# Moving parts of a chunked linear attention between four engines: scores to ScalarE and GpSimd, states and diagonals to VectorE

## The chip, the cores and the metric

The kernel runs on one core of a Trainium2 chip. The metric is device time in microseconds (us). The engines are TensorE (PE in the rows, its weight loads PEld), VectorE (DVE), ScalarE (ACT), GpSimd (POOL) and SyncE (SP), which issues nearly all loads and stores. Each engine works through its own queue in order and waits on semaphores for the others.

## The reference

Three layers follow each other. The first is a linear attention with a decaying state per head, the other two are feed-forward layers, the last one with a router over eight experts.

```python
# 4 batches, 8 heads, 768 steps, head size 48
for t in range(S):
    cur = einsum('bhd,bhe->bhde', u * k[t], v[t])
    y[t] = einsum('bhd,bhde->bhe', r[t], state + cur)
    state = w * state + einsum('bhd,bhe->bhde', k[t], v[t])
x = y as 3072 tokens x 384
h = x @ w_in                       # 384 -> 2048
g = h where h >= 1, 0 where h <= -1, else (h + 1)**2 / 4
x = g @ w_out                      # 2048 -> 384
# router: argmax of normalised x with 8 experts, gate = its softmax value
out = gate * (relu(x @ w1[e]) @ w2[e])   # 384 -> 1024 -> 384
```

## The kernel before

The 3072 tokens are 24 units of 128 steps, six to a batch. A unit works on its steps at once: the decay goes into r and k beforehand (`rk`), the scores of all steps with all steps are taken by TensorE (`s0`) into two PSUM tiles of 128x512 with four heads each, evacuated with a mask that keeps the steps before (`e0`, `e1`, function `s0_ev`), and multiplied with v (`s1`), to which the state of the unit before is added by further matmuls. What a step gives itself, the term with u, is the diagonal of the scores, a number per step and head (`dg`, `dg2`). For units below `DIAG` (8) it is multiplied with v apart (`dv`, on VectorE for the first four units and on GpSimd for units 4 to 7), and TensorE adds it into the output of `s1` by three transposes. For later units it is written into the diagonal of the masked scores by a predicated copy on VectorE (`dd`, function `s0_dg`, two instructions a unit), and the transposes fall away.

The state after a unit is the old one plus k times v, with the decay of 128 steps put on it. For units below `BY_PE` (5) TensorE also adds the old state, by a matmul with the identity, and ScalarE evacuates the sum with the decay as its scale (`s2p`). For later units TensorE gives only k times v, VectorE adds the old state in two instructions (`s2v`) and ScalarE puts the decay on in four (`s2w`). The last unit of a batch makes no state.

ScalarE and VectorE split the output of a unit into a high and a low part (`s3h`, `s3l`) for the first feed-forward layer, which takes three matmuls for each product. Six blocks of 512 tokens go through it in steps of 128 hidden columns: `h` on TensorE, four operations on ScalarE and one on VectorE, the low part `gl` on GpSimd, then `o` and `og` on TensorE. The weights come in as packed 64-bit numbers and are unpacked on the way, in three instructions on VectorE, one on ScalarE and one on GpSimd (`wlo`), in time for their first use. Units 0 to 7 are the first two blocks; later units are slipped in between the steps of earlier blocks.

The order on every engine is written out ahead by a planner, class `Schedule`. Each task has an engine, a modelled length (`COST`), what it depends on, what buffers it takes, and a due time. The planner goes forward in modelled time and gives an engine, of the tasks that are ready first, the one with the earliest due time. `SHIFT` adds an offset to the due time, by kind (`"e0"`), by unit or step (`"u3"`, `"k17"`) or by both (`"s1_u8"`). The PSUM tiles of the attention share five slots (`att`). Before the first matmuls that count, TensorE is kept busy by matmuls with the identity (L761).

Lines of the profile that the text names: `s0` L616 (units below 8) and L624, `e0`/`e1` L636, `dd` L653, `dv` L605, transposes of dv L694, `s1` L690, state by TensorE L715 and L720, without it L724, its evacuation L680, `s2v` L735 and L737, `s2w` L743, `rk` L541, `kk` L550, `ru` L566 and L568, `wlo` L481, `gl` L854.

Of the kernel before, what the change touches and what calls it, by code (L numbers as in the profile page):

```python
# [15 lines left out]
AF = mybir.ActivationFunctionType  # L16
ALU = mybir.AluOpType
# [7 lines left out]
C = 128  # L25
NU = NT // C
UPB = S // C
NP = H // 2
# [2 lines left out]
NF2 = F2 // 128  # L31
WARM = 9
RAMP = 4
DIAG = 8
HALVES = 2
ROLL = 8
W_LO, W_HI = 0.75, 1.3125
# [25 lines left out]
class Schedule:  # L63
# [47 lines left out]
    def run(self):  # L111
# [63 lines left out]

COST = {"wkc": 0.42, "s2p": 1.0, "dg": 0.12, "s3h": 0.4, "whi": 0.76, "relu": 0.59, "over": 0.53, "sqr": 0.53, "gh": 0.53,
# [58 lines left out]
def d_pe(n):  # L235
    return n / 2300 + 0.011


SHIFT = {"": 31.25, "az": 14, "b0": -19.75, "b1": -26, "b2": 4.5, "b3": 22.75, "b4": -30.5, "b5": 295.25, "dd":
# [15 lines left out]
         "le0": -5.75, "le1": -39.25, "le2": -6.75, "lka": 9.25, "lkl": -20.5, "lkm": -9.5, "look": -248.5, "max":  # L255
# [14 lines left out]
         46.25, "sm": 330, "sma": -190, "smc0": -63.25, "smc1": 0.25, "sqa": -87.25, "sqs": -32.25, "swd": -3.5,  # L270
# [8 lines left out]
         "whp": 6.5, "wkc": -2.75, "wkd": -3.25, "wkr": 6.75, "wl": 109.75, "wlo": 201.5, "wlp": -72.5, "wp1": 25.25,  # L279
         "wp2": 35.25, "wp3": 54.5, "x1ld": 28.75, "x2h": 30.5, "x2l": 36, "x2ld": -14.25, "xth0": -21, "xth1": 8,  # L280
         "xtl0": -57.75, "xtl1": -6.25, "xts0": -46.5, "xts1": -3.5, "xts2": -54.75, "xts3": 7.25, "z": 98.5, "zs":
         -119.75}
U_DVE, U_PE, W_DVE = 4.7, 3.5, 4.0
ON_DVE = {}
KK_PE, W_PSUM, G_PSUM, DV_PSUM, BY_PE = 2, 2, 0, 4, 5


@with_exitstack
def fused_kernel(ctx, tc, att, wcol, wrow, ub, ucol, win, wout, emb, tau, w1, w2, out):
    nc = tc.nc  # L290
# [42 lines left out]
    def bcast(ap, shape):  # L333
        return ap.to_broadcast(shape)
# [143 lines left out]
    def w_lo(c, eng=None):  # L478
# [8 lines left out]
                            channel_multiplier=-1)  # L487
# [26 lines left out]
    ats = [atp.tile([128, 2, NP, C], F32, name=f"at{i}") for i in range(2)]  # L514
# [6 lines left out]
    st = {}  # L521
# [110 lines left out]
    def s0_ev(u, j):  # L632
        s = st[u]
        at = s["at"] = ats[u % 2]
        if u < ROLL:
            nc.vector.tensor_tensor(out=at[:, j], in0=s["a"][j], in1=bcast(mask.unsqueeze(1), [128, NP, C]), op=ALU.mult)  # L636
        else:
            m = C // 2
            nc.vector.tensor_tensor(out=halves(at[:, j, :, m:]), in0=halves(s["a"][j][:, :, m:]),
                                    in1=bcast(sel[:, 0, :, m:].unsqueeze(2), [128, 2, NP // 2, m]), op=ALU.mult)  # L640
            for i in range(2):
                x, y = slice(m * i, m * i + m), slice(2 * i, 2 * i + 2)
                nc.vector.tensor_tensor(out=at[x, j, y, 0:m], in0=s["a"][j][x, y, 0:m],
                                        in1=bcast(sel[x, 0, i:i + 1, 0:m], [m, NP // 2, m]), op=ALU.mult)

    def s0_dg(u, j):
        s = st[u]
# [656 lines left out]
    add = sch.add  # L1304
# [23 lines left out]
    for u in range(NU):  # L1328
# [49 lines left out]
        e0 = add("e0", f"u{u}", "DVE", 0.68, lambda u=u: s0_ev(u, 0), [s0] + z + (sels if u >= ROLL else []), due - 9,  # L1378
                 alloc=[] if z else [atb], use=[a0] + ([atb] if z else []), after=e0s[u - 2:u - 1] if u > 1 else [])
        e0s.append(e0)  # L1380
        e1 = add("e1", f"u{u}", "DVE", 0.68, lambda u=u: s0_ev(u, 1), [s0, e0], due - 9, use=[a1, atb])
        if u >= DIAG:
            dv = dg
            for j in range(2):
                dv = add("dd", f"u{u}", "DVE", 0.62, lambda u=u, j=j: s0_dg(u, j), [e1, dv], due - 4.5, use=[atb, dgb])
        c = u % UPB
        s1 = add("s1", f"u{u}", "PE", (2.2 if c else 1.75) - 0.45 * (u >= DIAG), lambda u=u: (xt_tiles(unit_blk[u][0]), s1_pe(u)),
                 [e1, dv, l1, s2e.get(u - 1) if c else None, xhu.get(4 * m)], due - 1.5,
                 alloc=[yb] + (list(xbuf[m]) if i == 0 else []),
                 use=[ab, atb] + ([dvb] if u < DIAG else []) + ([state_b[u - 1]] if c else []) + (list(xbuf[m]) if i else []),  # L1390
                 after=[s1_of[u - 1]] if u else [])
# [562 lines left out]
```

## Time and profile before

| what | value |
| --- | --- |
| median of 3 runs | 710.27 us (709.94 to 710.44) |
| the profiled execution | 710.95 us |
| its span, first to last instruction | 709.1 us |
| granted clock of TensorE | 1.00 |
| TensorE busy | 699.4 us |
| VectorE busy | 450.4 us |
| ScalarE busy | 416.7 us |
| GpSimd busy | 304.8 us |

The profile is of one execution. Busy times are unions of the instructions of an engine. Matmuls are pipelined, their durations overlap and their ends are modelled, so the time that a group of them takes is read from its start to the start of the next group. The chain that ended last is followed back from the last instruction, at each step to what released it or to the instruction before it on its engine.

### The profile page before, as it was taken

The page shows a single profiled execution, that of the slowest core. Times are in us where ns is not written, and L with a number is a line of the kernel's source. Part 1 is how long each engine was busy: PE and PEld are TensorE (multiplying, and loading weights), DVE is VectorE, ACT ScalarE, POOL GpSimd, SP SyncE. Part 2 cuts the span into 40 slices and gives each one's busy share as a digit, 9 for nine tenths or more (in the row PEclk, how much of TensorE's full clock was granted, in tenths as well). Part 3 has the DMA queues.
Part 4 walks back from the last instruction along what each step waited for, and adds up shares of the span by engine and source line. Part 5 has one row for each costly group of instructions (what it writes and reads, how often), then busy time and mean ns, then how long its engine had stood idle before and what let it go on. Part 6 is the DMA issues. An engine that isn't in the chain of part 4 may idle for free.

```text
span 709.1 us, 14241 instructions
## 1 busy us (share of the span) xinstructions
PE 699.4 (99%) x5743; PEld 597.2 (84%) x5743; DVE 450.4 (64%) x842; ACT 416.7 (59%) x744; POOL 304.8 (43%) x251
## 2 busy tenths in 40 slices
PE   8999999999999999999999999999999999999997
PEld 7788888877888888887787888887899999999996
DVE  7989987699998313235994512121588586948664
ACT  3357777566556557765756866676566364625432
POOL 4699996574476522333622322234561121112100
PEclk9999999999999999999999999999999999999999
DMA  7866445254455105322642302000412021102011
GB/s 261 321 207 209 175 155 175 67 169 161 154 176 179 65 1 177 111 91 89 221 154 86 94 0 90 1 0 1 152 35 81 3 90 44 47 0 90 6 41 48
DMA packets 26136, 74.93 MB, mean 106 GB/s; under 512 B 2505, under 2 KB 9682, under 8 KB 26066
## 3 DMA queue, kind: packets, MB, share of 16 engines
q1 hardware_dynamic: 25778, 73.59, 30.8%
q8 instruction: 46, 0.75, 0.5%
q10 hardware_dynamic: 288, 0.39, 0.2%
q14 instruction: 24, 0.20, 0.1%
HBM read 62.74 MB, written 11.01 MB: 104 GB/s over the span
## 4 chain that ended last, share of the span: by engine, by line
PE 89%; DVE 4%; POOL 2%; DMA 2%; issue 1%; ACT 1%; POOLq 0%; DVEq 0%; SPq 0%
PE psh L341 9%; PE psh L343 9%; PE psh L342 9%; PE acc L876 9%; PE acc L879 9%; PE acc L877 9%; PE o L1246 5%; PE o L1243 5%; PE o L1244 5%; PE psm L341 4%; PE psm L342 4%; PE psm L343 4%; PE psy L690 3%; DMA attn<-att 2%; PE psa L624 2%; PE pslt L1009 1%
## 5 line engine op out<-in xcount | busy, mean ns | idle before, releaser
L854 POOL TENSOR_TENSOR gl<-a,gh 128x512 fp32r<-128x512 f32 (+1 forms) x98 | 136.8, 1397 | 185.5 <-ACT gh L849 171.5
L845 DVE TENSOR_TENSOR a<-psh,a 128x512 f32<-128x512 f32 (+1 forms) x98 | 66.5, 679 | 148.3 <-ACT a L842 146.5
L876 PE MATMUL acc<-gh,wout_h 128*128 128x512 f32 (+1 forms) x294 | 116.5, 398 | 0.1
L341 PE MATMUL psh<-xh,win_h 128*128 128x512 f32 (+1 forms) x294 | 115.6, 393 | 0.0
L343 PE MATMUL psh<-xh,win_l 128*128 128x512 f32 (+1 forms) x294 | 114.9, 391 | 0.0
L342 PE MATMUL psh<-xl,win_h 128*128 128x512 f32 (+1 forms) x294 | 114.9, 391 | 0.0
L877 PE MATMUL acc<-gh,wout_l 128*128 128x512 f32 (+1 forms) x294 | 114.5, 391 | 0.0
L835 ACT ACTIVATE a<-psh,half 128x512 f32<-128x512 f32 (+1 forms) x98 | 66.3, 676 | 73.1 <-PE psh L343 64.7
L849 ACT ACTIVATE gh<-a 128x512 fp32r<-128x512 f32 (+1 forms) x98 | 60.6, 620 | 42.4 <-DVE a L845 38.4
L1203 DVE TENSOR_TENSOR sc<-sc,psm 128x256 f32<-128x256 f32 x176 | 64.1, 417 | 30.5 <-PE psm L343 20.4
L879 PE MATMUL acc<-gl,wout_h 128*128 128x512 f32 (+1 forms) x294 | 82.3, 393 | 0.2 <-POOL gl L854 0.2
L876 PEld LDWEIGHTS acc<-gh,wout_h 128*128 128x128 f32 x294 | 55.2, 188 | 15.0 <-ACT a L842 1.0
L341 PEld LDWEIGHTS psh<-xh,win_h 128*128 128x128 f32 x294 | 55.2, 188 | 13.0 <-issue 0.2
L343 PEld LDWEIGHTS psh<-xh,win_l 128*128 128x128 f32 x294 | 55.2, 188 | 12.8
L342 PEld LDWEIGHTS psh<-xl,win_h 128*128 128x128 f32 x294 | 55.2, 188 | 12.5
L879 PEld LDWEIGHTS acc<-gl,wout_h 128*128 128x128 f32 x294 | 54.3, 188 | 13.3 <-POOL gl L854 0.4
L877 PEld LDWEIGHTS acc<-gh,wout_l 128*128 128x128 f32 x294 | 55.3, 188 | 11.9
L1243 PE MATMUL o<-w2h,gh 128*128 128x384 f32 x192 | 64.6, 336 | 0.0
L1244 PE MATMUL o<-w2l,gh 128*128 128x384 f32 x192 | 64.4, 336 | 0.0
L839 ACT ACTIVATE a<-a 128x512 f32<-128x512 f32 (+1 forms) x98 | 60.9, 621 | 2.5
L842 ACT ACTIVATE a<-a 128x512 f32<-128x512 f32 (+1 forms) x98 | 60.7, 619 | 2.2
L1218 ACT ACTIVATE gh<-sc 128x512 fp32r<-128x512 f32 x44 | 26.7, 627 | 47.2 <-DVE sc L1203 43.7
(218 smaller groups left out, 1387.3 us busy)
## 6 DMA issues: line engine op xcount, KB each, us to landing
att<-att SPq DMA_DIRECT2D x22, 736.0 KB, 5.1
w<-win SPq DMA_DIRECT2D x16, 768.0 KB, 5.2
w<-wout SPq DMA_DIRECT2D x16, 768.0 KB, 4.5
attn<-att SPq DMA_DIRECT2D x20, 384.0 KB, 3.9
x1d<-x SPq DMA_DIRECT2D x6, 768.0 KB, 4.8
x1f<-x1d SPq DMA_DIRECT2D x6, 768.0 KB, 5.8
out<-o SPq DMA_DIRECT2D x10, 384.0 KB, 2.9
hw<-w SPq DMA_DIRECT2D x8, 384.0 KB, 4.0
```

Source lines behind the costliest of these rows:

```text
L341: nc.tensor.matmul(o, lhsT=sh, rhs=mh, start=first, stop=False, skip_group_check=True)
L342: nc.tensor.matmul(o, lhsT=sh, rhs=ml, start=False, stop=False, skip_group_check=True)
L343: nc.tensor.matmul(o, lhsT=sl, rhs=mh, start=False, stop=last, skip_group_check=True)
L835: nc.scalar.activation(out=a, in_=hp, func=AF.Relu, bias=half[:, 0:1], scale=0.5)
L845: nc.vector.tensor_tensor(out=a if out is None else out, in0=hp, in1=a, op=ALU.max)
L854: (eng or nc.gpsimd).tensor_tensor(out=gl, in0=a, in1=gh.bitcast(F32), op=ALU.subtract)
L876: nc.tensor.matmul(o, lhsT=wh, rhs=gh, start=(f == f0 and c0 == 0), stop=False, skip_group_check=True)
L877: nc.tensor.matmul(o, lhsT=wl, rhs=gh, start=False, stop=False, skip_group_check=True)
L879: nc.tensor.matmul(o, lhsT=wh, rhs=gl, start=False, stop=(f == f1 - 1), skip_group_check=True)
L1203: nc.vector.tensor_tensor(out=out, in0=x, in1=bank[:, j], op=op)
L1243: nc.tensor.matmul(o, lhsT=gh[:, c], rhs=ws[2][:, f, :], start=(f == 0), stop=False, skip_group_check=True)
L1244: nc.tensor.matmul(o, lhsT=gh[:, c], rhs=ws[3][:, f, :], start=False, stop=False, skip_group_check=True)
```

## The change

Half of the scores of units 0 to 3, the four heads of `e1`, are evacuated by ScalarE as a plain copy (`ea`, new function `s0_copy`) and masked in place by GpSimd with an `affine_select` (`em`, new function `s0_mask`); `E_ACT` says for how many units. `BY_PE` goes from 5 to 3, so the states of units 3 and 4 take the form of the later units; `DIAG` goes from 8 to 6, so the diagonals of units 6 and 7 do. The wait of `s1` on `e0` is named beside that on `e1`. The small loads for the tables of the router (`mixl`) wait for `s1` of unit 5 in place of unit 7, as they follow `DIAG`. `COST` gets the two new kinds, and all of `SHIFT` is new; its values are left out here.

```diff
-DIAG = 8
+DIAG = 6
...
+"ea": 0.53, "em": 1.23,
...
-SHIFT = {"": 31.25, "az": 14, "b0": -19.75, "b1": -26,
...
+SHIFT = {"": 48.75, "az": 10.5, "b0": 14.25, "b1": -32,
...
+E_ACT = 4
 U_DVE, U_PE, W_DVE = 4.7, 3.5, 4.0
 ON_DVE = {}
-KK_PE, W_PSUM, G_PSUM, DV_PSUM, BY_PE = 2, 2, 0, 4, 5
+KK_PE, W_PSUM, G_PSUM, DV_PSUM, BY_PE = 2, 2, 0, 4, 3
...
+    def s0_copy(u, j):
+        nc.scalar.activation(out=ats[u % 2][:, j], in_=st[u]["a"][j], func=AF.Copy)
+
+    def s0_mask(u, j):
+        at = ats[u % 2][:, j]
+        nc.gpsimd.affine_select(out=at, in_=at, pattern=[[0, NP], [1, C]], compare_op=ALU.is_gt, fill=0.0, base=0, channel_multiplier=-1)
...
-        e1 = add("e1", f"u{u}", "DVE", 0.68, lambda u=u: s0_ev(u, 1), [s0, e0], due - 9, use=[a1, atb])
+        if u < E_ACT:
+            e1 = add("ea", f"u{u}", "ACT", 0, lambda u=u: s0_copy(u, 1), [s0, e0], due - 9, use=[a1, atb])
+            e1 = add("em", f"u{u}", "Pool", 0, lambda u=u: s0_mask(u, 1), [e1], due - 9, use=[atb])
+        else:
+            e1 = add("e1", f"u{u}", "DVE", 0.68, lambda u=u: s0_ev(u, 1), [s0, e0], due - 9, use=[a1, atb])
...
-                 [e1, dv, l1, s2e.get(u - 1) if c else None, xhu.get(4 * m)], due - 1.5,
+                 [e0, e1, dv, l1, s2e.get(u - 1) if c else None, xhu.get(4 * m)], due - 1.5,
```

## Rows read from the trace of the kernel before

**Rows 1.** The page: the span, and busy time, share and instructions of each engine.

```profile
span 709.1 us, 14241 instructions
PE 699.4 (99%) x5743; PEld 597.2 (84%) x5743; DVE 450.4 (64%) x842; ACT 416.7 (59%) x744; POOL 304.8 (43%) x251
```

**Rows 2.** Stretches: from:to, length, busy us of each engine (instructions), clock, DMA.

```profile
8.00:28.00 20.00, 18.67 (x311) 15.04 (x309) 19.14 (x32) 6.66 (x19) 8.67 (x8) 1.00 0.88 338
28.00:57.00 29.00, 28.73 (x516) 24.33 (x509) 25.82 (x44) 15.88 (x40) 27.43 (x27) 1.00 0.67 222
57.00:104.00 47.00, 47.00 (x206) 38.10 (x207) 42.41 (x38) 35.23 (x59) 44.98 (x28) 1.00 0.51 172
...
380.00:704.00 324.00, 323.76 (x1922) 291.48 (x1920) 174.64 (x397) 181.47 (x310) 87.93 (x77) 1.00 0.15 46
704.00:709.10 5.10, 0.00 (x0) 0.00 (x0) 0.59 (x1) 0.10 (x1) 0.00 (x0) 1.00 0.43 154
```

**Rows 3.** Waits of TensorE: line and what it waited for, total us, times, longest.

```profile
PE psy L694 <- DVE at L636: 0.7, 1, 0.7
```

**Rows 4.** The chain that ended last, in order of time: start us, us, what.

```profile
19.29 8.34 DMA attn<-att
...
51.24 0.69 POOL gl L854
...
52.90 2.02 POOL dv L605 x2
...
54.97 0.33 PE psy L694
```

**Rows 5.** Timeline of TensorE: start us, us, instruction, how many merged.

```profile
28.11 0.91 PE L715 MATMUL pskv<-state,ident 128*128 128x384 f32 x2
...
29.45 0.55 PE L694 MATMUL psy<-ident,dv 128*128 128x128 f32 x3
...
46.52 0.52 PE L724 MATMUL pskv<-att,kk 128*32 128x48 f32 x32
46.98 0.39 PE L876 MATMUL acc<-gh,wout_h 128*128 128x256 f32 x1
...
49.92 0.49 PE L694 MATMUL psy<-ident,dv 128*128 128x128 f32 x3
50.34 1.08 PE L690 MATMUL psy<-at,att 128*32 128x128 f32 x32
```

**Rows 6.** VectorE, 0 to 140 us, groups: count, busy us, mean ns, idle before.

```profile
L636 DVE TENSOR_TENSOR at<-psa,mask 128x512 f32<-128x512 f32 x16 | 10.3, 682 | 0.0
...
L735 DVE TENSOR_TENSOR state<-pskv,state 48x192 f32<-48x192 f32 x4 | 1.4, 352 | 4.5 <-PE pskv L724 4.4
```

**Rows 7.** Tile `at`: count, ns at least, median, most, first and last start.

```profile
L653 DVE COPY_PREDICATED at<-sel,dg x32: 722/760/2377, 135.7 to 370.3; 128x512 f32<-128x512 int32 x32
```

**Rows 8.** GpSimd, 0 to 140 us, groups, columns as in group 6.

```profile
L605 POOL TENSOR_TENSOR dv<-att,dg 128x256 f32<-128x256 f32 x4 | 4.8, 1191 | 0.0
...
L605 POOL TENSOR_TENSOR dv<-att,dg 128x128 f32<-128x128 f32 x4 | 2.4, 590 | 0.0
...
L486 POOL TENSOR_SCALAR_AFFINE_SELECT mask<-mask 128x128 f32<-128x128 f32 x1 | 0.3, 292 | 0.1
```

**Rows 9.** ScalarE, 0 to 140 us, groups, columns as in group 6.

```profile
L885 ACT ACTIVATE x<-acc 128x512 f32<-128x512 f32 x4 | 2.2, 596 | 0.1
```

**Rows 10.** Timelines of VectorE and GpSimd near 38 us, columns as in group 5.

```profile
38.02 1.21 DVE L541 TENSOR_TENSOR att<-att,pwt 128x1024 f32<-128x1024 f32 x1
...
36.98 1.01 POOL L566 TENSOR_TENSOR ru<-attn,ubt 128x384 f32<-128x384 f32 x1 [0.37 <-DVE dg L589]
38.07 2.04 POOL L568 TENSOR_TENSOR ru<-ru,attn 128x384 f32<-128x384 f32 x1
```

**Rows 11.** Timelines of GpSimd and TensorE near 60 us, columns as in group 5.

```profile
58.52 1.83 POOL L481 TENSOR_TENSOR wout_l<-sc,wout_h 128x768 fp32r<-128x768 f32 x1
...
62.26 0.40 PE L876 MATMUL acc<-gh,wout_h 128*128 128x512 f32 x1
```

More of the change, by code (lines that the diff above doesn't have):

```diff
@@ L236, in d_pe @@
     return n / 2300 + 0.011
-SHIFT = {"": 31.25, "az": 14, "b0": -19.75, "b1": -26, "b2": 4.5, "b3": 22.75, "b4": -30.5, "b5": 295.25, "dd":
[15 rows of a table removed]
-         "le0": -5.75, "le1": -39.25, "le2": -6.75, "lka": 9.25, "lkl": -20.5, "lkm": -9.5, "look": -248.5, "max":
[14 rows of a table removed]
-         46.25, "sm": 330, "sma": -190, "smc0": -63.25, "smc1": 0.25, "sqa": -87.25, "sqs": -32.25, "swd": -3.5,
[8 rows of a table removed]
[L279 to L282, printed above, removed]
+SHIFT = {"": 48.75, "az": 10.5, "b0": 14.25, "b1": -32, "b2": 8, "b3": 24.25, "b4": -39.75, "b5": 244.25, "dd":
[16 rows of a table added]
+         "lka": 12.5, "lkl": -20.5, "lkm": -25, "look": -239.5, "max": -71.75, "mixl": 33.75, "o": 294.5, "o2": 53.5,
[14 rows of a table added]
+         -9.25, "sm": 403.25, "sma": -190.75, "smc0": 0.75, "smc1": -37, "sqa": -1.5, "sqr": 15, "sqs": -2, "swh":
[8 rows of a table added]
+         0.5, "wkd": 14.25, "wkr": 110.5, "wl": 113.25, "wlo": 219.5, "wlp": -213.5, "wp1": 27.5, "wp2": -8.25,
+         "wp3": 139.5, "x1ld": 27.25, "x1st": 14.75, "x2h": 67.75, "x2l": 26.75, "x2ld": -19.25, "xth0": -33.25,
+         "xth1": 53.5, "xtl0": -132.75, "xtl1": 0.5, "xts0": -11, "xts1": 85.75, "xts2": -24, "xts3": 3.75, "z":
+         98.75, "zs": -147}
+E_ACT = 4
 U_DVE, U_PE, W_DVE = 4.7, 3.5, 4.0
 ON_DVE = {}
-KK_PE, W_PSUM, G_PSUM, DV_PSUM, BY_PE = 2, 2, 0, 4, 5
+KK_PE, W_PSUM, G_PSUM, DV_PSUM, BY_PE = 2, 2, 0, 4, 3
 @with_exitstack
```

77 rows, old and new, of tables (COST, SHIFT) are left out of this document.

## The prediction

> **What bounds the kernel now.** I read the page's totals first, then the busy time by stretch, then the waits of TensorE, then the chain that ended last, and only then single rows. The totals show TensorE busy for 699.4 us of a span of 709.1 [rows 1], so at most 9.7 us of the span are not its work. The stretches say where these lie [rows 2]: from 57 us to 704 us it has next to no idle time, after 704 us come 5.1 us of evacuation and stores that the change does not touch, from 8 to 28 us it is idle for 20 - 18.67 = 1.33 us, and from 28 to 57 us for 0.27 us. The rest lies ahead of 8 us, where nothing of this change runs. So the time is the start, TensorE's own work, some 1.6 us of waits in the attention of the first two blocks, and the tail. A change can win by taking work off TensorE, or by taking away these waits; it can lose only by making new ones.
>
> The same two stretches show how little room the others have there [rows 2]. VectorE is busy for 19.14 of 20 us and then 25.82 of 29; GpSimd for only 8.67 of 20, but then 27.43 of 29, and 44.98 of 47 after that; ScalarE for 6.66 of 20 and 15.88 of 29. The longest wait of TensorE in the first stretch, 0.7 us, ends with VectorE's masking of scores [rows 3]. The chain that ended last runs up to 55 us through others: 8.34 us of a load that lands at 27.6 us, and in its last piece GpSimd's gl, kk and then 2.02 us of dv of unit 7, which releases the transposes of that unit [rows 4]. From there on it is TensorE. So up to 55 us several engines are near their limit at once, and an order of the work has to suit all of them.
>
> **The change, part by part. TensorE.** With `BY_PE` 3 the states of units 3 and 4 are no longer carried by TensorE. For unit 3 this group starts at 28.11 us with the identity matmul and the next one, the transposes, at 29.45: 1.34 us. The form without the identity starts at 46.52 us for unit 6, and the next matmul at 46.98: 0.46 us [rows 5]. Unit 4 repeats unit 3, so the saving is 2 x 0.88 = 1.76 us. With `DIAG` 6 the three transposes of dv of units 6 and 7 go; those of unit 6 take from 49.92 to 50.34 us [rows 5], 0.42 us, twice 0.84. Together TensorE loses 2.60 us, all of it inside a stretch in which it is never idle for long. I count from start to start, since the durations in the rows overlap.
>
> **VectorE.** It loses the second half of the masks of units 0 to 3, 4 x 0.68 = 2.73 us [rows 6], all before 28 us. It gains two adds for each of two states, 4 x 0.35 = 1.42 us [rows 6], and four predicated copies for the diagonals of units 6 and 7. The trace has these copies only for later units: 0.72 us at best, 0.76 in the median, 2.38 at worst [rows 7]. I take 0.76, the median of 32, and keep 2.38 for the bound: 3.04 us, up to 9.5. The sum is +1.73 us by 57 us, against 0.86 + 3.18 = 4.04 us of idle time in the two stretches. It fits, though from 28 to 57 us alone +4.46 does not fit into 3.18; the 2.73 us won before 28 us must be used to bring work forward.
>
> **GpSimd.** It loses dv of units 6 and 7, 2 x (1.19 + 0.59) = 3.56 us [rows 8], where it is fullest. It gains four masks on 128x512. The nearest row is the same operation on 128x128, 0.29 us [rows 8]; the price lies between that and four times that, 1.17, and I take 1.17, as the whole of such an operation grows with the elements at the worst. That is 4.7 us ahead of 28 us, in 11.3 us of idle time. **ScalarE** gains four copies of a 128x512 tile of PSUM, 0.60 us each [rows 9], 2.4 us in 13.3 us of idle time, and the two states cost it as much as before, since it scales them either way.
>
> **New waits.** The second half of the scores of units 0 to 3 now goes s0, e0 on VectorE, copy on ScalarE, mask on GpSimd, and the copy waits for e0 as the code has it, so the halves do not run beside each other. After e0 come 0.60 + 1.17 us and two hand-overs, in place of 0.68. Behind the copy in ScalarE's queue are the evacuations of y and the scaling of the states; behind the mask on GpSimd is kr of the next unit, on which TensorE's diagonal matmuls wait. This costs nothing while TensorE has the next unit's s0, dg or s2 to do, some 3 us a unit; if that cover is gone, 1.2 us. The state of unit 3 now reaches ScalarE through two more instructions, 0.7 us later; TensorE has s1 of unit 3 and s0 of a later unit to do before unit 4 needs it, so I take it at nothing. The three small loads of the tables may leave SP's queue two units earlier; they are tiny and wait for nothing else.
>
> **What is late next.** TensorE arrives at unit 7 at 51.9 us in place of 54.54 if all 2.60 us come through. Its dv, which ended there at 54.9, is gone. The next release after that is `out1`, the low part of a weight: GpSimd ends it at 58.52 + 1.83 = 60.35 us, and it is used at 62.26 [rows 11], 1.9 us of slack for 2.60 us of gain. But ahead of it on GpSimd stood dv of unit 7 [rows 4], which is gone. So I take this stall at nothing, bound 0.7 us.
>
> **The order.** The new due offsets reorder every queue, and the trace of before cannot show the new order. I bound it by its own idle time: at best the 1.6 us of waits before 57 us vanish too; at worst nothing ahead of 55 us gets shorter, and the 2.60 us turn into waits. I take it at zero: waits on VectorE before 28 us should shrink, those on it after 28 us should grow.
>
> **One rule against it.** GpSimd's product of 128x384 took 1.01 us alone and 2.04 us when VectorE's product of two SBUF tensors began at 38.02 us just ahead of it [rows 10]. The Trainium skill, SBUF — State Buffer, section "SBUF: two separate sides", calls the port pair that VectorE and GpSimd share an exclusive lock: the one that starts first holds it for its whole instruction, and the other stands still. The trace agrees, with 1.03 us for one meeting. By that rule moving a mask from VectorE (which read PSUM and one SBUF tensor) to GpSimd, and putting predicated copies beside a full GpSimd, makes more such meetings; it is rival three below.
>
> **The sum.** The median of the runs is 710.27 us; the profiled execution took 710.95 with a span of 709.1, so 1.8 us lie around the span and it is 0.7 us above the median, and I apply the difference to the median. 710.27 - 1.76 - 0.84 = 707.67, forecast 707.7 us.
>
> **Rivals.** (1) *The chain up to 55 us holds.* For: it runs through a load that is late, VectorE and GpSimd, all near full [rows 2, 4]. Against: GpSimd loses 3.56 us exactly there. Then only what hung on dv of unit 7 is won, 0.3 us: 710.0 us. (2) *The halves in a row.* If unit 0, the first with nothing else ready, waits for copy and mask, the 1.2 us above come once: 708.9 us. (3) *Slower: the shared access.* If each of the four copies for the diagonals meets a GpSimd instruction and takes 0.76 + 1.03 (2.04 - 1.01 [rows 10]), and each of the four masks costs a VectorE instruction as much, VectorE has +1.73 + 8 x 1.03 = 10.0 us by 57 us against 4.0 us of room: 5.9 us late, less the 2.6 us that TensorE saves, is 713.6. It decides where the meetings cost more than 4.04 - 1.73 + 2.60 = 4.9 us, that is from five of the eight on; with six or seven it is about 712. Against it: GpSimd is under half busy while the masks run [rows 2].
>
> **Chances and range.** Forecast 0.60 (its own range 706.0 to 708.7, from the bound of 1.6 us below and some new waits above), rival one 0.21, rival two 0.10, rival three 0.09. The low end is 707.67 - 1.6 = 706.1, less a little for a shorter start, 705.9; the high end takes in rival one: 710.2. A measurement of this kernel tells about 0.2%, 1.4 us, from no change. Faster by that means under 708.85: the forecast and half of rival two, 0.65; within it: rival one and the other half, 0.26; slower: rival three, 0.09.
>
> **What would show it.** The identity matmul on the state falls from 10 to 6 instructions and the transposes of dv from 24 to 18; TensorE's busy time falls by about 2.6 us with the span. If the busy time falls and the span does not, waits before 57 us have grown, and the stretches say on whom: on GpSimd's mask in 8 to 28 us (rival two), on VectorE's predicated copies or GpSimd in 28 to 57 us (rivals one, three). Predicated copies above 1 us in the mean speak for rival three. The forecast is wrong too if the new order opens waits after 57 us, where before there are almost none.

## The result and the profile after

The changed kernel takes 718.33 us in the median of four runs (716.11 to 718.35) against 710.34 for the kernel before on the same chip: 1.0106 times as long, with an interval of 1.0086 to 1.0125. The forecast was 707.7, faster. The profiled execution took 716.11 us; its span is 5.3 us longer than that in [rows 1]. It was the fastest of the four, so its trace shows 5.3 of the 8.0 us. The helper functions are longer by two to nine lines, so L616 is now L618, L636 is L638, L653 is L660, L690 is L699, L694 is L703, L720 is L729, L724 is L733, L735 is L744; the new copy and mask are L649 and L653.

The page of the changed kernel: the span, and busy time and instructions of each engine.

```profile
span 714.4 us, 14349 instructions
PE 703.8 (99%) x5797; PEld 600.3 (84%) x5797; DVE 454.1 (64%) x846; ACT 418.4 (59%) x748; POOL 308.3 (43%) x251
```

The changed kernel by stretch, as [rows 2]: length, then busy us of PE, PEld, DVE, ACT and POOL.

```profile
8.00:28.00 20.00, 19.61 (x317) 15.87 (x317) 18.55 (x28) 9.12 (x24) 13.92 (x12) 1.00 0.90 328
28.00:57.00 29.00, 27.38 (x413) 24.50 (x416) 27.36 (x43) 14.79 (x37) 25.64 (x23) 1.00 0.54 172
```

TensorE's busy time rose by 4.4 us where it should have fallen by 2.6 [rows 1]. The work did fall. Counted from the start of one matmul to the start of the next, the identity matmuls went from 4.17 us (10) to 2.51 (6) and the transposes of dv from 3.83 us (24) to 2.92 (18), 2.56 us together. But the keep-warm matmuls (L770), which the kernel issues where it expects TensorE to wait, went from 5.34 us (30) to 10.88 (62). They count as busy. The timeline of the changed kernel's TensorE shows them:

```profile
32.70 2.72 PE L770 MATMUL wu<-mask,ident 128*128 128x128 f32 x22
35.97 0.69 PE L703 MATMUL psy<-ident,dv 128*128 128x128 f32 x3 [0.55 <-POOL dv L607]
...
38.25 0.94 PE L770 MATMUL wu<-mask,ident 128*128 128x128 f32 x6
39.44 2.06 PE L618 MATMUL psa<-att 64*128 64x128 f32 x32 [0.25 <-issue]
41.42 0.39 PE L343 MATMUL psh<-xh,win_h 128*128 128x256 f32 x1
```

The first `h` starts at 41.42 us. In the kernel before it was this row:

```profile
37.60 0.39 PE L341 MATMUL psh<-xh,win_h 128*128 128x256 f32 x1
```

Two queues meet in that gap. GpSimd, in the changed kernel:

```profile
26.86 1.63 POOL L653 TENSOR_SCALAR_AFFINE_SELECT at<-at 128x512 f32<-128x512 f32 x1
28.86 1.00 POOL L568 TENSOR_TENSOR ru<-attn,ubt 128x384 f32<-128x384 f32 x1 [0.37 <-POOL at L653]
30.70 1.01 POOL L552 TENSOR_TENSOR kk<-attn,wk 128x384 f32<-128x384 f32 x1 [0.84 <-PE psy L703]
31.67 1.02 POOL L570 TENSOR_TENSOR ru<-ru,attn 128x384 f32<-128x384 f32 x1
...
34.31 1.96 POOL L607 TENSOR_TENSOR dv<-att,dg 128x256 f32<-128x256 f32 x2
```

The last mask ends at 28.5 us, `kk` of unit 5 then waits 0.84 us at the head of the queue, the second product of `ru` of unit 4 stands behind it, and the first piece of dv of unit 4, on which TensorE waits, ends only at 35.9. And VectorE:

```profile
29.83 0.73 DVE L744 TENSOR_TENSOR state<-pskv,state 48x192 f32<-48x192 f32 x2
...
35.83 0.73 DVE L744 TENSOR_TENSOR state<-pskv,state 48x192 f32<-48x192 f32 x2
36.59 1.03 DVE L447 SCALAR_TENSOR_TENSOR psw<-w,psw 128x256 uint32<-128x256 uint32 x2
...
39.25 1.01 DVE L463 TENSOR_TENSOR win_l<-psw,win_h 128x256 fp32r<-128x256 f32 x2
```

The additions of the states of units 3 and 4 stand in front of the last unpacking of the first weights, which ended at 36.4 us before and ends at 40.3 now. Both times that is 1.2 us ahead of the first `h`, so it is not the last thing that `h` waits for: in TensorE's own queue `s0` of units 5 and 6 now stand in front of it, from 39.44 us on, where that of unit 6 came behind the first matmuls of `h` in the kernel before (39.93).

Behind 142 us, where no unit that the change touches is left, new waits of TensorE have come in place of two of 0.5 and 0.3 us: line, what it waited for, total us, times, longest.

```profile
PE psy L699 <- ACT a L851: 0.8, 1, 0.8
PE acc L885 <- ACT gh L858: 0.4, 1, 0.4
PE psm L343 <- DVE sc L1212: 0.2, 1, 0.2
```

To see where time is lost I add up, for each trace, what every step from one matmul's start to the next exceeds the median step of its shape in the trace of the kernel before, with the fillers counted whole. What is left is work. All numbers in us, one profiled execution each:

| kernel | to 57 us | 57 to 142 | from 142 | work | last matmul starts |
| --- | --- | --- | --- | --- | --- |
| before | 25.7 | 1.6 | 43.9 | 630.3 | 703.6 |
| after | 26.5 | 4.8 | 47.0 | 628.7 | 708.9 |

The levels mean little, since every switch between tiles is in them, but the differences do: work -1.6 (the removed matmuls count here at the median step of their shape alone, which is less than the 2.56 us from start to start), up to 142 us +4.0, behind it +3.1. The border at 57 us is not to be read by itself: `s1` of late units came behind it, and 2.2 us of the +3.2 between 57 and 142 us are its steps, of which the kernel before has none there.

### The profile page after: what moved, and what is told of

It is laid out like the page before. It is cut to its first block, busy times and chain, and to the rows that moved or that the text cites. A ratio compares the mean times of both kernels' runs of the same rounds, so it can differ in the third digit from the quotient of the medians.

```text
span 714.4 us, 14349 instructions
## 1 busy us (share of the span) xinstructions
PE 703.8 (99%) x5797; PEld 600.3 (84%) x5797; DVE 454.1 (64%) x846; ACT 418.4 (59%) x748; POOL 308.3 (43%) x251
## 4 chain that ended last, share of the span: by engine, by line
PE 93%; POOL 3%; DVE 1%; ACT 1%; DMA 1%; issue 1%; POOLq 0%; ACTq 0%; DVEq 0%
PE psh L343 9%; PE acc L885 9%; PE psh L345 9%; PE psh L344 9%; PE acc L888 9%; PE acc L886 9%; PE o L1255 5%; PE o L1252 5%; PE o L1253 5%; PE psy L699 4%; PE psm L343 4%; PE psm L344 4%; PE psm L345 4%; PE psa L626 2%; PE psa L618 1%; PE wu L770 1%
```

## The experiments

**Theory A**, the forecast's: TensorE's work is the time, so the moves are sound, and if the time rises, the new due offsets did it. **Theory B**: in the first 57 us other engines set the pace too, and what comes off TensorE there comes back as waits. I count differences from the median of the kernel before on the same chip.

### One move at a time, at the old order

The planner's choice is replaced by a fixed order: every engine takes its tasks in the order of the start times that the planner gave in the kernel before (`PIN`), and new tasks stand where the replaced ones stood (copy and mask at `e1`, the additions at `s2p`, the diagonal copies when `dg2` and `e1` are done).

```diff
     def run(self):
+        for t in self.tasks:
+            n = count[t.kind, t.item] = count.get((t.kind, t.item), -1) + 1
+            place[t] = self.place(t.kind, t.item, n)
+            lists[t.eng].append(t)
+        for q in lists.values():
+            q.sort(key=lambda t: -place[t])
...
-                t = min((t for r, t in rs if r <= t0), key=lambda x: x.due)
+                r = self.ready(q[-1])
```

`ord_diag` has only `DIAG` 6, `ord_state` only `BY_PE` 3, `ord_scores` only `E_ACT` 4, `ord_all` all three.

> The order of the kernel before is kept on every engine, with the old due offsets out of play; only DIAG goes from 8 to 6. The four predicated copies stand on VectorE where both the diagonal and the scores are made. Theory A (the moves are sound, the new due offsets made the waits): TensorE's saving of 0.84 us comes through, about 709.5 us. Theory B (up to 57 us VectorE and GpSimd set the pace, work taken off TensorE comes back as waits, and what is added to VectorE delays the chain): not faster than before, 710.3 to 712.5 us, TensorE's waits between 28 and 57 us up by 1 to 3 us.

Measured: 710.82 us (709.84 to 712.02) against 710.35, +0.5; ratio 1.0007, interval 0.9997 to 1.0016.

> The order of the kernel before on every engine; only BY_PE goes from 5 to 3, the two adds of a state stand on VectorE where ScalarE's evacuation of that state stood. Theory A: the saving of 1.76 us comes through, about 708.5 us. Theory B: 710.3 to 713 us, with waits of TensorE between 28 and 57 us up by 2 to 4 us, since the unpacking of the first weights on VectorE comes later by the time of the adds (0.7 us a unit).

Measured: 711.17 us, +0.8; ratio 1.0013, interval 1.0003 to 1.0022.

> The order of the kernel before on every engine; only E_ACT goes from 0 to 4, copy and mask stand on ScalarE and GpSimd where the second mask stood on VectorE. Nothing is taken off TensorE. Theory A: VectorE has 2.7 us less to do before 28 us, so no loss, 709.5 to 710.5 us. Theory B: the second half waits for the first, for ScalarE and for GpSimd, some 1.5 to 2.5 us more a unit where nothing else is ready: 711.5 to 714 us, with the first matmul of the feed-forward layer 1 to 3 us later than 37.6 us.

Measured: 711.01 us, +0.7; ratio 1.0011, interval 1.0001 to 1.0021.

> The order of the kernel before on every engine with all three moves. Theory A: 707.7 us, as forecast, so that the new due offsets alone made the loss. Theory B: the sum of the three single moves, 712 to 717 us, about as the changed kernel with its own offsets.

Measured: 713.20 us (712.99 to 713.70), +2.9; ratio 1.0041, interval 1.0027 to 1.0055.

No move wins. Together they cost more than the sum of the three medians, 2.0 us, though the interval of `ord_all`, 1.9 to 3.9 us, reaches down to it. Its trace has a wait of 0.6 us on the low part of a weight that none of the three single runs has:

```profile
PE acc L839 <- POOL wout_l L436: 0.6, 1, 0.6
```

The work did come off (transposes -1.10 us in `ord_diag`, identity matmuls -1.69 in `ord_state`). VectorE's timeline of `ord_state` shows what the states move, with lines of that kernel: the addition stands in front of the unpacking, which starts 0.83 us later than the 35.44 us of the kernel before.

```profile
35.51 0.73 DVE L697 TENSOR_TENSOR state<-pskv,state 48x192 f32<-48x192 f32 x2
36.27 1.02 DVE L416 TENSOR_TENSOR win_l<-psw,win_h 128x256 fp32r<-128x256 f32 x2
```

That the kernel rises by the same 0.8 us does not follow from these rows. The unpacking ends at 37.3 us, and the first `h` starts at 37.69, 0.09 us later than before, right behind `s1` and without a wait. Where the 0.8 us are lost is open.

One rival is untested. The planner writes fillers where its model expects TensorE to wait: 12 more in `ord_state`, 18 in `ord_scores`, 30 in `ord_all`, none in `ord_diag`. They can delay TensorE themselves. These are rows of `ord_scores`:

```profile
19.63 1.61 PE L723 MATMUL wu<-mask,ident 128*128 128x128 f32 x12
21.07 0.49 PE L656 MATMUL psy<-ident,dv 128*128 128x128 f32 x3
21.49 0.86 PE L652 MATMUL psy<-att,state 128*32 128x128 f32 x24
22.17 1.06 PE L652 MATMUL psy<-at,att 128*32 128x128 f32 x32
```

The mask that the last row reads ends at 21.03 us, before the fillers are through. No run left the new fillers out, so the 2.9 us are the price of the moves together with their fillers. Theory A falls here; B fits the moves, but its mechanism is not shown by these runs. And 2.9 us are not 8.0.

### What the order costs

`after_2` is the changed kernel once more.

> The changed kernel once more, unedited, with a profile of another execution. The profiled execution so far took 716.1 us, the three others 718.3. If the difference lies in the starting phase (the granted clock rose at 7.7 us there), the spans of this run scatter between 714 and 717 us and the time of the first h matmul of the profile (41.4 us) scatters with them. If it lies behind it, the first h matmul stays within 0.5 us and the time from it to the last matmul moves. Expected for the median: 718.3 us.

Measured: 717.66 us (715.66 to 718.63), +7.4; the first `h` at 41.5 us in a span of 715.4. So of the 1.0 us between the two profiled spans 0.1 lies ahead of the first `h`; what the scatter of 3 us comes from stays open.

`new_order` and `split142` hold other orders in the same way: the first that of the changed kernel with `E_ACT` 0 and `BY_PE` 5, the second as below, where `BEF` and `AFT` are the start times that the planner gave in the kernel before and in the changed one.

```diff
 PIN = {task:
-    BEF[task]
+    AFT[task] if AFT[task] < 142 else 1000 + BEF[task]
 for task in tasks}
```

> The order of the changed kernel held on every engine, but two of its three moves undone: the second halves of the scores of units 0 to 3 are masked by VectorE again, where ScalarE's copy stood, and the states of units 3 and 4 carried on by TensorE again, with the evacuation where ScalarE's decay stood; the diagonals of units 6 and 7 stay with VectorE. If the new order is sound and pays only with the moves (theory A turned round), the kernel loses what the moves save, some 2 us: 720 us or more. If the order itself costs, whatever is moved (theory B), it stays within 1 us of the changed kernel: 717.5 to 719.5 us.

Measured: 716.84 us (716.44 to 718.10), +6.6. Two moves undone at the new order win 0.8 to 1.5 us by the medians, near the 0.8 + 0.7 that they cost at the old one, but the runs overlap (716.44 to 718.10 against 715.66 to 718.63), so this cannot be told from none. Shown is that undoing them does not cost the 2 us or more by which an order made for the moves would have paid.

> All three moves; the order of the changed kernel for what it starts before 142 us, and the order of the kernel before for all that comes later. In the traces, TensorE's steps from one output tile to another behind 142 us are 193 in the kernel before and 207 in the changed one, and cost 5.8 and 8.8 us above the usual step; two waits of 0.6 and 1.0 us at 169 and 177 us are among them. If that part of the order costs, the time falls by 2.5 to 3.5 us against the changed kernel, to 715 or 716 us. If all of the loss was made before 142 us, it stays at 718 us.

Measured: 713.62 us (711.71 to 715.00), +3.4; ratio 1.0047, interval 1.0032 to 1.0061. Against the changed kernel 4.0 to 4.7 us are back, more than expected, and the time is that of `ord_all` within 0.4. Its waits of TensorE behind 142 us are one:

```profile
PE psy L692 <- DVE a L847: 0.5, 1, 0.5
```

In the sums of steps `split142` has 43.2 us from 142 us on and `ord_all` 44.0, like the 43.9 of the kernel before; the changed kernel has 47.0, `after_2` 48.0 and `new_order` 47.5. About 0.9 us of this is in the waits shown. Most of the rest is in steps from one output tile to another: the changed kernel has 207 of them, `split142` 194, and without the waits they cost 2.2 us more above the median step, 0.17 us for each one more. `psy` to `psa` comes three times with 0.59 us in all, where `split142` has none. `acc` to `psy` comes five times with 1.36 us, but 0.99 of these are one step that holds the wait on `a` shown above; the other four cost 0.09 us each, as the one in `split142` does. The new order slips attention units between steps of the feed-forward layer at other places and more often, and TensorE pays for each switch.

So the 8 us are: the moves with their fillers 2.9 (`ord_all`), the new order up to 142 us 0.4, which is less than these runs scatter, and the new order behind it 4.0 to 4.7.

### What holds the first 57 us

These kernels leave work out of the kernel before, with its order as it is. `pe_less` leaves out two of three transposes of units 0 to 7:

```diff
-            for kk in range(KD):
+            for kk in (KD - 1,):
...
-start=(kk == 0)
+start=True
```

> The kernel before with two of the three transposes of each of units 0 to 7 left out, so that the diagonal of the scores reaches only part of the output; the last transpose stays, and with it the wait for dv. Nothing else is moved or added. 24 transposes take 3.83 us there, start to start, so 16 of them are 2.55 us of TensorE's work. Theory A, on which the forecast was built (TensorE's work is the time): 707.8 us. Theory B (up to 57 us VectorE, GpSimd and ScalarE set the pace): 709.5 to 710.4 us, and the time turns up again as fillers and waits.

Measured: 710.85 us, +0.6; ratio 1.0007, interval 0.9997 to 1.0017. The saving was less than written, 1.98 us (3.83 to 1.84), since a transpose that stands alone takes 0.23 and not 0.16. Nothing of it reached the end. From start to start, the steps of the state matmuls behind it grew by 1.20 us and those of the first layer by 0.48. The waits of TensorE up to 142 us name some of it: the 0.7 us of [rows 3] are gone, but the first of these was 0.4 in the kernel before, that on `gl` 0.2, and that on GpSimd's dv not there:

```profile
PE psa L616 <- PE pskv L720: 0.9, 2, 0.6
PE acc L879 <- POOL gl L854: 0.7, 1, 0.7
...
PE psy L694 <- POOL dv L605: 0.3, 1, 0.3
```

That is the plainest case against the forecast: TensorE alone was relieved, nothing was added, its fillers are the 30 of the kernel before, and the time did not fall. `vec_less` leaves out `e1` of units 0 to 3, `pool_less` the second product of `ru` of units 4 to 7; `two_less` is both, `three_less` both with `pe_less`; `vec_late` and `three_late` have units 3 to 6 in place of 0 to 3.

```diff
-lambda u=u: s0_ev(u, 1), [s0, e0]
+lambda u=u: u < 4 or s0_ev(u, 1), [s0, e0]
...
-at[:, h % 2, h // 2, :]
+at[:, h % 2 if u > 3 else 0, h // 2, :]
...
-lambda u=u: prep_ru(u, 1), [ru0]
+lambda u=u: u < 8 or prep_ru(u, 1), [ru0]
```

> The kernel before with the second half of the scores of units 0 to 3 left out on VectorE (four instructions of 0.68 us, 2.73 us): the masked scores of four heads never exist, and TensorE reads those of the other four heads twice, so its work is the same. Nothing takes the work over. If VectorE sets the pace up to 57 us, this is the most that the change could gain by moving the masks, and the time falls by 1.0 to 2.7 us, to 707.6 to 709.3. If GpSimd or the loads set it, it stays at 710.3, within 0.4 us, and then the change had nothing to gain there. Theory A gives no change either, since TensorE's work is the same.

Measured: 709.77 us, -0.6; ratio 0.9998, interval 0.9987 to 1.0009. It lies between what the two readings expected: 2.7 us less on VectorE cannot be told from none. (One of the ten runs took 712.39, so the ratio is nearer to 1 than the medians.)

> The kernel before with the second product of ru left out on GpSimd for units 4 to 7 (1.01, 0.99, 2.04 and 1.80 us, 5.84 us), so that the diagonal of their scores lacks the factor k. Nothing takes the work over. If GpSimd sets the pace from 28 to 57 us, the time falls by 1 to 4 us, to 706.3 to 709.3. If VectorE or the loads do, it stays at 710.3, within 0.4 us.

Measured: 709.37 us, -1.0; ratio 0.9987, interval 0.9978 to 0.9997. The low end of what was expected, for 5.84 us of work.

> The two omissions at once: the second half of the scores of units 0 to 3 on VectorE and the second product of ru of units 4 to 7 on GpSimd (2.73 and 5.84 us). If the two engines take turns at the end of the path, so that relief on one alone is lost to the other, this gains more than the two runs of one omission together. If one of them sets the pace alone, it gains what that run gains. If the loads do, it stays at 710.3.

Measured: 708.73 us, -1.6; ratio 0.9981, interval 0.9972 to 0.9991. The sum of the two runs with one omission, no more.

> The two omissions and, as a third, two of the three transposes of units 0 to 7 (2.55 us of TensorE's work). Theory B says that TensorE's work counts only where the others have been relieved: by 1.0 to 2.55 us below the run with two omissions. If it is equal to that run within 0.5 us, something else than these three engines still holds the start, the loads for instance.

Measured: 708.96 us, -1.4; ratio 0.9980, interval 0.9970 to 0.9989. TensorE's relief is worth nothing here either.

`load_more` makes the loads of `attn` for units 2 and 3 longer:

```diff
-            n = DM if u < RAMP else 2 * DM
+            n = 2 * DM
```

> The kernel before with the loads of attn for units 2 and 3 twice as long (192 KB more each, 384 KB), the added half never read. No instruction is added. The page shows 321 and 338 GB/s near there, so the loads behind them land some 1.2 us later. If the loads are one of the things that hold the start (the run with three omissions gained nothing over the one with two, and the load of attn that lands at 27 us stood in its chain), the time rises by 0.6 to 1.2 us, to 711 to 711.5. If not, it stays at 710.3.

Measured: 710.25 us, -0.2; ratio 1.0000, interval 0.9990 to 1.0009. These loads are not what holds the start.

> The kernel before with the second half of the scores of units 3 to 6 left out on VectorE, in place of units 0 to 3: again four instructions, 2.7 us, TensorE's work unchanged. In the trace of the kernel before VectorE stands idle for 0.25 us in all between 26.6 and 43.1 us, where the first weights are unpacked and where the change puts its two additions of the states. If that stretch of VectorE sets the pace, the same 2.7 us is worth more here than in units 0 to 3 (0.6 us there): 707.5 to 709.0 us. If VectorE has no part in it, 709.7 to 710.3.

Measured: 709.53 us, -0.9; ratio 0.9993, interval 0.9983 to 1.0002. Again between the two readings: 0.3 us more than `vec_less` gave, which cannot be told from none.

> As the run with three omissions, but with the scores of units 3 to 6 in place of those of units 0 to 3: VectorE 2.7 us, GpSimd 5.84 us, TensorE 2.55 us less. If VectorE's stretch from 27 to 43 us is what kept the run with three omissions at 709.0, this falls below it, by up to the 2.55 us of TensorE, to 706.4 to 708. If it stays at 709, what holds the start has not been found.

Measured: 709.28 us, -1.1; ratio 0.9989, interval 0.9979 to 0.9998. It does not fall below `three_less`, so VectorE from 27 to 43 us alone is not what kept that run up. The chains that ended last differ. In `three_less` the chain goes through a load of `attn` and then through VectorE, with pieces of it from 29 to 38 us, among them:

```profile
19.19 7.67 DMA attn<-att
...
29.58 0.94 DVE psw L445 x2
30.51 1.49 DVE att L541
32.00 0.47 DVE xl L754
32.47 1.19 DVE at L636 x2
33.67 0.93 DVE win_l L461 x2
```

In `three_late`, where units 0 to 2 keep their masks, it goes through VectorE from 7.6 to 22.6 us, among them:

```profile
18.15 1.19 DVE at L636 x2
...
20.28 1.19 DVE at L636 x2
21.47 1.14 DVE att L541
22.83 1.28 POOL kr L573
24.16 1.05 PE psdg L579 x8
```

I read this as two stretches of VectorE that end nearly together, so that relief in one shows the other. It is a reading of two chains: a run with both relieved, and TensorE besides, was not made. The load in the chain of `three_less` is a rival: `load_more` speaks against it in the kernel before, but no run moved that load in `three_less`. Shown is that relief of TensorE, VectorE or GpSimd alone gives back little or nothing of what was left out, and that TensorE's work up to 57 us is not the time. ScalarE was not relieved.

### Offsets searched anew

Were the offsets of the change only badly chosen for its structure? `best_all` is the changed kernel, `best_bef` the old structure, `best_scores` the move of the scores alone, each with `SHIFT` found by random steps over the planner's modelled end, equally long for each.

```diff
-SHIFT = {"": 48.75, "az": 10.5, "b0": 14.25, "b1": -32,
+SHIFT = {...}
```

> The changed kernel, all three moves, with due offsets of its own, searched anew for this structure by random steps over the planner's modelled end. Theory B says that the moves gain nothing at an order made for the kernel without them, and cost 2.9 us there; whether an order made for them changes that is open. If the new offsets of the change were merely badly chosen and the moves are sound (theory A), this falls below the kernel before, to 708 to 709.5 us. If the moves themselves cost, it stays above, at 711 to 714.

Measured: 715.00 us (714.00 to 717.18), +4.6; ratio 1.0070, interval 1.0042 to 1.0097.

> The structure of the kernel before, none of the three moves, with due offsets searched in the same way and for as long. It is what the run with all moves and searched offsets has to be held against. Expected 708 to 710 us: the offsets alone move the time by some us either way, and this one should lie below the run with all moves by what the moves cost (theory B, 2 to 3 us) or above it (theory A).

Measured: 711.93 us (710.79 to 712.96), +1.5; ratio 1.0022, interval 1.0012 to 1.0032. The search did not beat the offsets of the kernel before.

> Only the move of the scores (copy by ScalarE, mask by GpSimd, units 0 to 3), with offsets searched in the same way. At the order of the kernel before this move cost 0.7 us. Theory B: within 1 us of the run of the old structure with searched offsets.

Measured: 712.34 us (710.55 to 714.56), +1.9; ratio 1.0031, interval 1.0016 to 1.0046. Level with `best_bef`, as expected.

Between `best_all` and `best_bef` lie 3.1 us, but that is not a price of the moves. In the sums of steps `best_all` loses 3.6 us more behind 142 us (47.8 against 44.2) and 2.2 more before it (29.9 against 27.7), for 1.8 us less work. Up to 142 us the moves come out 0.4 us behind there, and the rest lies where the two differ in order alone. No run had the moves and a gain; that none can exist is not shown.

## Why the prediction was wrong

- **The work: right.** States and transposes were forecast at -2.60 us and measured at -2.56 (-1.66 and -0.90).
- **"So the time is the start, TensorE's own work", waits and the tail: wrong up to 57 us.** The sum let all of the 2.60 us reach the end. At the order of before the same three moves gave +2.9 us (`ord_all`), 5.5 us off. `pe_less`, which takes 1.98 us off TensorE and adds nothing, gave +0.6: the saving came back as waits in the steps of the state matmuls and of the first layer.
- **"I take it at zero", the order: wrong, and a miss of like size.** Its bounds, -1.6 to +2.60 us, came from the stretch up to 57 us. But all of the offsets were new, and the order behind 142 us cost 4.0 to 4.7 us (`split142`). The last sentence of the prediction named new waits behind 57 us as what would make it wrong; no price was put on them.
- **"It fits", VectorE: wrong.** The sum itself, +1.73 us, was fair: the busy time of VectorE in the two stretches rose by 0.95 us. But 4.04 us of idle time in 49 is an average. In the kernel before VectorE stands idle for 0.25 us between 26.6 and 43.1 us, in this row, and the two additions fall there:

```profile
30.88 0.55 DVE L589 TENSOR_REDUCE dg<-ru 128x8 f32<-128x384 f32 x1 [0.25 <-POOL ru L568]
```

- **The prices.** A tile `at` in the changed kernel: count, ns at least, median and most.

```profile
L649 ACT ACTIVATE at<-psa x4: 597/598/599, 10.4 to 25.0; 128x512 f32<-128x512 f32 x4
L653 POOL TENSOR_SCALAR_AFFINE_SELECT at<-at x4: 630/1294/1629, 12.6 to 26.9; 128x512 f32<-128x512 f32 x4
L660 DVE COPY_PREDICATED at<-ident,dg x4: 962/1612/2080, 48.5 to 62.9; 128x512 f32<-128x512 int32 x4
```

  The copy was sized right at 0.60 us. The mask has a mean of 1.21 against 1.17, though two of four are above the bound. The predicated copies have a mean of 1.57 us against the 0.76 taken, within the bound of 2.38. The row of 0.76 came from units behind 135 us; from 142 to 380 us GpSimd is busy for 108.68 of 238 us, from 28 to 57 us for 27.43 of 29 [rows 2].
- **"I take this stall at nothing", the low part of a weight:** right in the changed kernel. In `ord_all` TensorE waited 0.6 us on it, near the bound of 0.7, without having gained 2.60 us.
- **Rival three, slower: right in sign, wrong in kind.** The meetings are real. The longest copy runs beside this product on GpSimd, VectorE's row first:

```profile
50.32 2.08 DVE L660 COPY_PREDICATED at<-ident,dg 128x512 f32<-128x512 int32 x1
...
49.98 1.82 POOL L483 TENSOR_TENSOR win_l<-sc,win_h 128x768 fp32r<-128x768 f32 x1
```

  Together the four are 3.4 us above the best such copy (4 x 1.57 - 4 x 0.72). The Trainium skill, SBUF — State Buffer, section "SBUF: two separate sides", lets the one that starts first keep the shared port pair for its whole instruction. The trace agrees in size: the product ends at 51.8 us, and 0.72 us more would be 52.5, where the copy ends at 52.4. But with the order of before, `ord_diag` has the same copies at 1.17 to 1.55 us and loses only 0.5 us.
- **Rival one, the chain up to 55 us holds: the nearest for each move, and it had 0.21.** It priced the gain at 0.3 us. The runs with one move came out at +0.5 to +0.8. That this is the work which the moves put on the other engines is argued, not shown. `pe_less` is the rival in its pure form.
- **Rival two, the halves in a row:** 1.2 us were taken for the worst. `ord_scores` lost 0.7, with 2.05 us of fillers more; how much of the 0.7 is the fillers is open.
- **How it would show:** the counts of 6 and 18 came as written. That the busy time falls by 2.6 us did not, because fillers are matmuls; the sign to look for was their number.

## What to carry to other kernels

Before work is taken off a busy engine, leave some of it out in a run and see whether the time falls: `pe_less` took 1.98 us off TensorE for nothing, which was reason enough to doubt the two moves that take work off it. Idle time helps only where the new instruction will stand, so read the timeline of the engine at that place and not its share of a stretch. And a new order written by a planner is a change of its own, to be tried apart from the edit that came with it, over the whole kernel and not only near the edit.

## What the runs showed of the hardware

One program does not start alike each time. These are rows of TensorE's timeline in two executions of the changed kernel, first the one profiled first, then `after_2`:

```profile
6.01 1.06 PE L776 MATMUL pstw<-ident,pwt 128*128 128x128 f32 x4
6.87 1.91 PE L770 MATMUL wu<-mask,ident 128*128 128x128 f32 x12
8.61 0.60 PE L557 MATMUL pskk<-ident,att 128*128 128x128 f32 x4
```

```profile
5.96 0.66 PE L776 MATMUL pstw<-ident,pwt 128*128 128x128 f32 x4 [0.26 <-DVE half L520]
6.45 1.50 PE L770 MATMUL wu<-mask,ident 128*128 128x128 f32 x12
7.79 0.60 PE L557 MATMUL pskk<-ident,att 128*128 128x128 f32 x4
```

The same matmuls take longer in the first, and the first useful one starts 0.82 us later. In both TensorE runs fillers from 2.02 us on, and the step from one of them to the next halves, from 0.213 to 0.111 us: at 7.72 us in the first and at 4.95 in the second. There it goes from the lower to the higher of its two clock levels (1.2 and 2.4 GHz). The stretches give a granted clock of 1.00 from the start in both, but the trace's record of the clock begins only at 7.71 and 5.00 us; in the kernel before it begins at 6.00. What sets the moment is open. It is no effect of the change, and it is not the scatter of the time: the later start belongs to the shorter span, 714.4 us against 715.4.

A step of TensorE from `acc` to `psy` cost 0.09 us above the usual one in either order, a step from `psy` to `psa` 0.20 us (0.59 in three).
